# Late work of VectorE offered later, gate rows on GpSimd's queue, and p of group 3 scaled in the f stage

## The chip, the cores and the metric

The kernel runs on one core of a Trainium2 chip. The metric is the device time of one execution in microseconds (us). Three runs of the kernel before gave a median of 733.19 us (730.4 to 735.96).

## The reference

Two blocks read the same x (2048 tokens of 640 features) and are mixed by a gate of each token:

```python
g = sigmoid((x * gate_w).sum(-1))                      # one number per token
q, k, v = x @ wqkv                                     # 32 heads of 20
pq, pk = phi(q), phi(k)       # phi(t) = where(t > 0, t + 1, exp(t)) + 1e-6
kv = sum_s pk[s] v[s]^T ;  z = sum_s pk[s]             # per head
o = (pq @ kv) / (pq . z + 1e-6)
a = o @ wo
b = (sigmoid(x @ w_gate) * (x @ w_up)) @ w_down        # 1536 wide
out = g * a + (1 - g) * b
```

All of it is float32. The kernel gets that accuracy from split operands: each operand is a high part and a low part, and a product is three matmuls (lines 417 to 419), with a single one here and there (line 428).

## The kernel before

Tokens are handled in four groups of 512 (0 to 3), features in chunks of 128. "p" is phi(q) without its 1e-6, kept in DRAM as p_dram (128 features x 5 chunks x 4 groups x 512 tokens). kv and wo are multiplied together early into one 640 x 640 matrix M, so that the first block is a = M^T (p + 1e-6) scaled, per token and head, by the factor g / (pq . z + 1e-6).

Stages in the order of time: the k side (to about 145 us), the q side of groups 2 and 3, the gated unit of groups 2 and 3 (an "f stage"; twelve steps f, each 128 wide), the q side of groups 0 and 1, the f stage of groups 0 and 1 (some 450 to 645 us, `f_phase(0, ...)`), and the tail (from some 645 us), which forms M^T p for groups 2 and 3, then for 0 and 1, adds the gated unit's share and stores the result.

In the second f stage VectorE also does work that no matmul of that stage needs:

- `queue_dens` (lines 1575 to 1631) finds the factors, first for groups 2 and 3 (queued at step 2), then for 0 and 1 (at step 7). For each group it loads the five chunks of p (tile pden), sums p z into the tile fac (`one`), stores that in den_dram, loads it back turned so that heads lie along partitions (`turn_in`, four loads a group, which also loads the gate row gs), adds the parts, takes the reciprocal and multiplies by the gate (`factor`), stores the result in fac_dram, and loads it back spread over the 128 feature rows (`turn_out`, four loads a group). In the kernel before, the gate rows and the spreading loads are issued on SyncE's queue (SP), the rest on GpSimd's (POOL).
- `queue_m` forms the high and low parts of M (tiles mr, mt) and stores them through GpSimd's queue; its next loads of M (mr from m_dram) go on SyncE's queue.
- `queue_e` (lines 1435 to 1447) makes three small corrections of a step's weights (tile ws, 128 x 128 each).

In the tail `load_p` brings p of a group back from p_dram, `queue_scale` multiplies each chunk by the factor (`pq_scale`, one VectorE instruction of 128 x 512 a chunk), `queue_pq` splits it in a high part (ScalarE) and a low part (VectorE), and `queue_pt` forms sums of four chunks and splits those too. `queue_seed` puts the gated unit's share times 1 - g (tile omg) into a PSUM tile (dd or rot), on top of which the matmuls add. `load_m(1)` brings three of the ten pieces of M.

The order of the work is not written out by hand where it is queued: `Order` keeps an estimate of TensorE's, ScalarE's and VectorE's time while the program is written, and after each block of matmuls `fill` takes from its queues what is ready and fits (lists in the order urgent, streams, items, lazy, chain, spare; `chain` holds `queue_dens`, `spare` holds `queue_m`). Ready is what `ready()` says: for a transfer, the landing that `Rings` estimates for it. `DEN_LAG` (5.0) is added to that estimate in some places. `need` emits a queued piece at once. So a piece is emitted where the estimate says its data has landed; on the chip each engine runs its instructions strictly in that order, and an instruction whose data is late holds everything behind it on its engine. A tile name has a fixed number of buffers, so a load waits until the earlier user of its buffer is done. All vector, scalar and DMA instructions stand in helpers, so that their lines are those of the helpers: 433 ScalarE, 437, 441, 443 to 448 VectorE, 374 DMA.

Of the kernel before, what the change touches and what calls it, by code (L numbers as in the profile page):

```python
# [10 lines left out]
OP = mybir.AluOpType  # L11
# [3 lines left out]
P = 128  # L15
S, D, F = 2048, 640, 1536
H, DH = 32, 20
KC = D // P
FC = F // P
LAST = FC // 2 - 1  # L20
TG = 512
# [7 lines left out]
EPS = 1e-6  # L29
# [285 lines left out]
DEN_LAG = 5.0  # L315
# [65 lines left out]
def v_cost(w):  # L381
    return 0.07 + w / 960

@with_exitstack
def gated_mix_kernel(ctx: ExitStack, tc: tile.TileContext, x0, xt, xn, wk, wv, wo, wst_q, wst_f, out_t):
# [6 lines left out]
    order = Order()  # L392
# [46 lines left out]
    def vec3(out, a, scalar, b, op0, op1, after=""):  # L439
        order.on_vec(width(out), after, 1.0, out, a, b)  # L440
        nc.vector.scalar_tensor_tensor(out, a, scalar, b, op0=op0, op1=op1)
# [17 lines left out]
    def add(out, a, b, after=""):  # L459
        vec2(out, a, b, OP.add, after)  # L460
# [792 lines left out]
    def tt(name, dt=F32, shape=(P, TG)):  # L1253
        return pw.tile(list(shape), dt, name=name, tag="t", bufs=4)
# [180 lines left out]
    def queue_e(f):  # L1435

        n = ("f", 0, f)
        d, u = EW[f, "d"], EW[f, "u"]
        dh, dl = d[:, :P], d[:, P:]
        uh, ul = (W[n, 1][c][:, 2 * P:] for c in range(2))  # L1440

        def fn():
            vec3(u[:, :P], f32(dh), -1 / UP, f32(ul), OP.mult, OP.add)
            vec3(u[:, P:], f32(ul), UP, f32(uh), OP.mult, OP.add)
            vec3(dl, f32(dh), 1 / UP, f32(dl), OP.mult, OP.add)
        order.add(0, 3 * v_cost(P), fn, ("e", f), lambda: max(order.when(d), order.when(WT[n, 1])),
                  stream=("e", f), due=order.due((0, f, 3)))

    def queue_et(late):
# [112 lines left out]
    def gate_store():  # L1562
# [9 lines left out]
                              t[b * H:b * H + n, 1])  # L1572
        sp.dma_start(gate_rep, gate_dram[0].rearrange("(i o p) -> i o p", o=1, p=P).broadcast_to([n, H, P]))

    def queue_dens(*gs2):

        nonlocal fac
        if "f" in EF:
            EF.pop("f")
            fac = fac_tile()  # L1580
        st = {}

        def load(g, u):
            if u < KC:
                st[g, u] = tt("pden")
                gp.dma_start(st[g, u], p_dram[:, u, g])
                st["at", g, u] = lambda: order.when(st[g, u])

        def one(g, u):
            td = fac[:, g]  # L1590
            if u == 0:
                vec1(td, st[g, u], zcol[:, 0:1], zeps[:, 0:1], OP.mult, OP.add)
            else:
                vec3(td, st[g, u], zcol[:, u:u + 1], td, OP.mult, OP.add)
            load(g, u + 2)
            if u == KC - 1:
                gp.dma_start(den_dram[:, g], td)
                st["at", g, u + 1] = lambda: order.when(den_dram[:, g])

        def turn_in(g):  # L1600
            for j in range(4):
                js = slice(j * H, (j + 1) * H)
                gp.dma_start(fac[js, g].rearrange("h (d c) -> h d c", c=P),
                                  den_dram[:, g, j * P:(j + 1) * P].rearrange("(d h) c -> h d c", h=H))
            st[g, "gs"] = tt("gs")[:, :P]
            sp.dma_start(st[g, "gs"], gate_rep[4 * g:4 * g + 4].rearrange("i h c -> (i h) c"))
            st["at", g, KC + 1] = lambda: max(order.when(fac[:, g]), order.when(st[g, "gs"]))

        def factor(g):
            td = fac[:, g]  # L1610
            q = td[:, :P]
            add(td[:, :2 * P], td[:, :2 * P], td[:, 2 * P:])
            add(q, q, td[:, P:2 * P])
            order.on_vec(5 * P, "")
            nc.vector.reciprocal(q, q)
            vec2(q, q, st[g, "gs"], OP.mult)
            gp.dma_start(fac_dram[:, g], q)
            st["at", g, KC + 2] = lambda: order.when(fac_dram[:, g])

        def turn_out(g):  # L1620
            for d in range(4):
                sp.dma_start(fac[d * H:(d + 1) * H, g].rearrange("h (j c) -> h j c", c=P),
                                  fac_dram[:, g].rearrange("(j h) c -> h j c", h=H))
        order.add(0, 0, lambda: [load(g, u) for u in range(2) for g in gs2], chain=True)
        for u in range(KC):
            for g in gs2:
                order.add(0, v_cost(TG), lambda g=g, u=u: one(g, u), None, lambda g=g, u=u: st["at", g, u]() + DEN_LAG, chain=True)
        for n, (v, fn) in enumerate(((0, turn_in), (2.0, factor), (0, turn_out))):
            for g in gs2:
                order.add(0, v, lambda g=g, fn=fn: fn(g), ("fac", g) if n == 2 else None,  # L1630
                          lambda g=g, n=n: st["at", g, KC + n](), chain=True)

    sp.t = max(sp.t, gp.cell[0])
    load_w()
# [457 lines left out]
    OMG = {}  # L2092
# [527 lines left out]
    def load_m(i):  # L2620

        while any(it[3] == "m" for it in order.spare) or order.pend:
            order.need("m")
            order._flush()
        n = (0, 7, 10)
        t = (wf_tile, ws_tile)[i]().rearrange("p a b -> p (a b)")[:, :(n[i + 1] - n[i]) * D]
        for j0, j1 in ((0, 4), (4, 7), (7, 10))[2 * i:2 + i]:
            sp.dma_start(f32(t[:, (j0 - n[i]) * D:(j1 - n[i]) * D]),
                         mp_dram.rearrange("p a b c -> p (a b c)")[:, j0 * D:j1 * D])
        for j in range(n[i], n[i + 1]):  # L2630
            MHL[divmod(j, 2)] = t[:, (j - n[i]) * D:(j - n[i] + 1) * D]
# [23 lines left out]
    def load_p(g):  # L2655

        if g == groups[0]:
            PL[g] = [tt("pl") for _ in range(KC - 1)]
            PL[g].append(f32(wu_tile()).rearrange("p a b -> p (a b)")[:, :TG])
            for u in range(KC):  # L2660
                sp.dma_start(PL[g][u], p_dram[:, u, g])
        else:
            PL[g], PL[g, "t"] = [], []
            for u in range(0, KC, 2):
                t = (x2_tile if g == groups[1] else h_tile)(dt=F32)
                w = min(2, KC - u)
                sp.dma_start(t[:, :w], p_dram[:, u:u + w, g])
                PL[g] += [t[:, i] for i in range(w)]
                PL[g, "t"].append(t)
        PL[g, "at"] = lambda: max(order.when(t) for t in PL[g])  # L2670
# [26 lines left out]
            ST[-1] = n = n()  # L2697
        return n

    def pq_scale(g, u):  # L2700
        p = PL[g][u]
        vec3(p, p, EPS, fac[:, g], OP.add, OP.mult)

    def pq_tiles(g):

        t = [x2_tile("pq", F32R) for _ in range({2: 4, 3: 2}.get(g, KC))]
# [7 lines left out]
    def queue_scale(g, lazy=False):  # L2714
        order.need(("fac", g), False)
        for u in range(KC):
            order.add(0, v_cost(TG), lambda u=u: pq_scale(g, u), ("sc", g), lambda: PL[g, "at"](), lazy=lazy)

    def queue_pq(g):

# [48 lines left out]
        vec2(ps, BL[g][o], OMG[g], OP.mult)  # L2769

    def b_at(g, o):
        return max(order.when(BL[g][o]), order.when(OMG[g]) if g in OMG else 1e9)

    def queue_seed(g, o, tag):
        order.add(0, v_cost(TG), lambda: seed_b(g, o, tag), ("b", g, o), lambda: b_at(g, o), first=True)
# [153 lines left out]
    pq_tiles(2)  # L2929
    queue_pq(2)  # L2930
    load_p(3)
    load_m(1)
    pq_tiles(3)
    queue_scale(3)
    queue_pq(3)
    load_b(2)
    load_omg(3)
    load_b(3)
    load_b(0)
# [105 lines left out]
```

## Time and profile before

| | us |
|---|---|
| median of three runs | 733.19 |
| the profiled execution's own time | 734.18 |
| its span, first to last instruction | 732.5 |
| TensorE busy (98% of the span) | 721.5 |
| VectorE busy (80%) | 589.2 |
| ScalarE busy (50%) | 366.1 |
| GpSimd busy (16%) | 118.0 |

Some 1.7 us of the execution lie outside the span. The profile names TensorE's matmuls PE, its weight loads PEld, VectorE DVE, ScalarE ACT, GpSimd POOL and SyncE SP; SPq and POOLq are the DMA queues of the last two. A row of the timeline has start, duration, engine, line, operation, output and inputs with their shape, and in brackets the engine's idle time before it and what ended that. Matmuls of 512 columns start some 0.23 us apart, while a row shows each as 0.39 us long, because they are pipelined. The granted clock of TensorE (PEclk) is 1.00 at full speed.

### The profile page before, as it was taken

The numbers are of one execution on the slowest core, as the hardware profiler recorded it, in microseconds if no ns is written. First come the engines' busy times: TensorE is split into PE (matmuls) and PEld (weight loads), VectorE is DVE, ScalarE is ACT, GpSimd is POOL, SyncE is SP. The second block draws the span as 40 slices with busy tenths as digits, with TensorE's granted clock in tenths as the row PEclk, the third lists the DMA queues.
The fourth block names the chain that finished last, engine by engine and source line by source line (L and its number), as shares of the span: only waits on it lengthen the run. The fifth ranks groups of instructions, "written<-read, shape, count | busy, mean of one in ns | idle before, by whom it ended". The sixth has DMA issues, their size and how long they took to land.

```text
span 732.5 us, 9922 instructions
## 1 busy us (share of the span) xinstructions
PE 721.5 (98%) x3401; PEld 607.3 (83%) x3401; DVE 589.2 (80%) x1045; ACT 366.1 (50%) x682; POOL 118.0 (16%) x199
## 2 busy tenths in 40 slices
PE   9999999999999999999999999998999999999898
PEld 8999999888888888888888888886788888887676
DVE  4988878987777889888998886665776888689886
ACT  5764749267557644444456762363332333335351
POOL 0311111113212211211121122013001131000200
PEclk9999999999999999999999999999999999999999
DMA  8474658698787856657688787889588897779623
GB/s 269 116 205 112 177 137 259 158 326 297 278 323 258 308 205 230 244 221 263 246 330 277 218 287 271 325 283 316 190 250 296 284 323 247 256 287 330 124 42 130
DMA packets 75657, 177.60 MB, mean 242 GB/s; under 512 B 12266, under 2 KB 34170, under 8 KB 73430
## 3 DMA queue, kind: packets, MB, share of 16 engines
q1 hardware_dynamic: 55654, 104.03, 43.5%
q0 software_dynamic: 19664, 72.70, 29.0%
q8 instruction: 27, 0.44, 0.2%
q10 hardware_dynamic: 288, 0.23, 0.1%
q14 instruction: 24, 0.20, 0.1%
HBM read 104.62 MB, written 67.33 MB: 235 GB/s over the span
## 4 chain that ended last, share of the span: by engine, by line
PE 92%; DVE 3%; DMA 2%; ACT 1%; issue 1%; POOL 0%; SPq 0%; DVEq 0%; POOLq 0%; ACTq 0%
PE ch L418 10%; PE ch L419 10%; PE ch L417 10%; PE cc L418 7%; PE cc L419 7%; PE cc L417 7%; PE dd L417 7%; PE dd L418 7%; PE dd L419 7%; PE rot L419 5%; PE rot L418 5%; PE rot L417 5%; PE ch L428 1%; PE cc L428 1%; DMA fac<-den_dram 1%; DMA omg<-gate_dram 1%
## 5 line engine op out<-in xcount | busy, mean ns | idle before, releaser
L437 DVE TENSOR_TENSOR hf<-c,hf 128x512 fp32r<-128x512 f32 x77 | 52.6, 687 | 26.0 <-ACT hf L433 25.5
L433 ACT ACTIVATE hf<-c 128x512 fp32r<-128x512 f32 (+1 forms) x79 | 48.8, 625 | 39.6 <-DVE c L437 39.6
L433 ACT ACTIVATE c<-ch 128x512 f32<-128x512 f32 x43 | 25.7, 597 | 77.8 <-PE ch L428 56.9
L417 PE MATMUL ch<-xth,ws 128*128 128x512 f32 x108 | 42.2, 391 | 0.0
L419 PE MATMUL ch<-xth,ws 128*128 128x512 f32 x108 | 42.1, 390 | 0.0
L418 PE MATMUL ch<-xtl,ws 128*128 128x512 f32 x108 | 42.1, 389 | 0.0
L437 DVE TENSOR_TENSOR tb<-rot,tb 128x512 f32<-128x512 f32 x60 | 39.0, 684 | 1.9 <-PE rot L419 1.9
L437 DVE TENSOR_TENSOR c<-cc,c 128x512 f32<-128x512 f32 x38 | 26.2, 688 | 17.0 <-ACT c L433 10.1
L437 DVE TENSOR_TENSOR c<-c,c 128x512 f32<-128x512 f32 x48 | 33.0, 688 | 2.6 <-ACT c L433 2.0
L437 DVE TENSOR_TENSOR tb<-dd,tb 128x512 f32<-128x512 f32 x41 | 28.1, 686 | 8.3 <-PE dd L419 8.3
L433 ACT ACTIVATE dd<-ch 128x512 f32<-128x512 f32 x22 | 12.8, 583 | 36.2 <-PE ch L428 20.4
L433 ACT ACTIVATE c<-dd 128x512 f32<-128x512 f32 x21 | 12.5, 597 | 35.6 <-PE dd L428 17.0
L417 PE MATMUL dd<-xrh,wg 128*128 128x512 f32 x73 | 28.7, 394 | 1.5 <-ACT dd L433 1.5
L437 DVE TENSOR_TENSOR wst<-wst 128x256 f32<-128x256 f32 (+2 forms) x69 | 27.4, 412 | 1.4
L418 PE MATMUL dd<-xrl,wg 128*128 128x512 f32 x73 | 28.4, 390 | 0.0
L419 PE MATMUL dd<-xrh,wg 128*128 128x512 f32 x73 | 28.4, 389 | 0.0
L417 PE MATMUL cc<-xbh,ws 128*128 128x512 f32 x71 | 27.6, 389 | 0.0
L418 PE MATMUL cc<-xbl,ws 128*128 128x512 f32 x71 | 27.6, 389 | 0.0
L419 PE MATMUL cc<-xbh,ws 128*128 128x512 f32 x71 | 27.6, 389 | 0.0
L433 ACT ACTIVATE c<-c 128x512 f32<-128x512 f32 x31 | 19.5, 628 | 10.5 <-DVE c L437 10.2
L433 ACT ACTIVATE cx<-ch 128x512 f32<-128x512 f32 x16 | 9.6, 597 | 29.1 <-PE ch L419 28.9
L419 PEld LDWEIGHTS ch<-xth,ws 128*128 128x128 f32 x108 | 20.3, 188 | 4.5 <-DVE ws L437 0.3
(755 smaller groups left out, 2403.2 us busy)
## 6 DMA issues: line engine op xcount, KB each, us to landing
wf<-ws POOLq DMA_DIRECT2D x12, 1152.0 KB, 7.7
wst<-wst_f SPq DMA_DIRECT2D x12, 640.0 KB, 4.9
wf<-wg POOLq DMA_DIRECT2D x12, 640.0 KB, 6.8
wd<-wd POOLq DMA_DIRECT2D x12, 640.0 KB, 8.1
wg<-wf SPq DMA_DIRECT2D x12, 640.0 KB, 6.2
wf<-wd SPq DMA_DIRECT2D x10, 640.0 KB, 7.8
ws<-wf SPq DMA_DIRECT2D x23, 256.0 KB, 4.8
xnst<-xn SPq DMA_DIRECT2D x16, 320.0 KB, 4.1
```

What stands on the lines that cost most here:

```text
L417: nc.tensor.matmul(out, l_hi, r_hi, start=first, stop=False, skip_group_check=True)
L418: nc.tensor.matmul(out, l_hi, r_lo, start=False, stop=False, skip_group_check=True)
L419: nc.tensor.matmul(out, l_lo, r_hi, start=False, stop=last, skip_group_check=True)
L428: nc.tensor.matmul(out, w, x, start=False, stop=n == len(singles) - 1, skip_group_check=True)
L433: nc.scalar.activation(out, src, fn, **kw)
L437: nc.vector.tensor_tensor(out, a, b, op=op)
```

## The change

Four things are changed:

1. Three ready times are put later: `queue_e` by 5.0 us of the estimate, the first step of `factor` by 5.0, and the seeds (`b_at`) by 2.5 behind their omg. `factor` is cut in two: the additions (`factor`) and then reciprocal, product and store (`turn_over`), each queued for both groups in turn.
2. The gate rows gs and the spreading loads of `turn_out` are issued on GpSimd's queue, no longer on SyncE's.
3. For group 3 the five chunks of p are loaded again in the f stage once the factor is there (four into pden tiles, the fifth into the part of fac that later serves group 0), multiplied by the factor, and stored back to p_dram through GpSimd's queue (`scale`). `load_p(3)` then loads p already scaled, and the tail's `queue_scale(3)` is gone.
4. `load_m(1)` is issued behind `load_b(2)`, no longer ahead of it.

```diff
@@ queue_e
-        order.add(0, 3 * v_cost(P), fn, ("e", f), lambda: max(order.when(d), order.when(WT[n, 1])),
+        order.add(0, 3 * v_cost(P), fn, ("e", f), lambda: max(order.when(d), order.when(WT[n, 1])) + DEN_LAG,
                   stream=("e", f), due=order.due((0, f, 3)))
@@ ahead of queue_dens
+    scaled = (3,)
+
+    def pq_scale(p, g):
+        vec3(p, p, EPS, fac[:, g], OP.add, OP.mult)
@@ queue_dens
-        def load(g, u):
+        def load(g, u, t=None):
             if u < KC:
-                st[g, u] = tt("pden")
+                st[g, u] = tt("pden") if t is None else t
                 gp.dma_start(st[g, u], p_dram[:, u, g])
                 st["at", g, u] = lambda: order.when(st[g, u])
...
-            sp.dma_start(st[g, "gs"], gate_rep[4 * g:4 * g + 4].rearrange("i h c -> (i h) c"))
+            gp.dma_start(st[g, "gs"], gate_rep[4 * g:4 * g + 4].rearrange("i h c -> (i h) c"))
...
             add(td[:, :2 * P], td[:, :2 * P], td[:, 2 * P:])
             add(q, q, td[:, P:2 * P])
+
+        def turn_over(g):
+            q = fac[:, g, :P]
             order.on_vec(5 * P, "")
             nc.vector.reciprocal(q, q)
             vec2(q, q, st[g, "gs"], OP.mult)
             gp.dma_start(fac_dram[:, g], q)
-            st["at", g, KC + 2] = lambda: order.when(fac_dram[:, g])
+            st["at", g, KC + 3] = lambda: order.when(fac_dram[:, g])
 
         def turn_out(g):
             for d in range(4):
-                sp.dma_start(fac[d * H:(d + 1) * H, g].rearrange("h (j c) -> h j c", c=P),
+                gp.dma_start(fac[d * H:(d + 1) * H, g].rearrange("h (j c) -> h j c", c=P),
                                   fac_dram[:, g].rearrange("(j h) c -> h j c", h=H))
+        def scale(g, u):
+            t = st[g, u]
+            pq_scale(t, g)
+            gp.dma_start(p_dram[:, u, g], t)
+
+        def scale_at(g, u):
+            return max(order.when(st[g, u]), order.when(fac[:, g])) + DEN_LAG
+
...
-        for n, (v, fn) in enumerate(((0, turn_in), (2.0, factor), (0, turn_out))):
+        for g in gs2:
+            st["at", g, KC + 2] = lambda: 0.0
+        for n, (v, fn) in enumerate(((0, turn_in), (0.6, factor), (0.9, turn_over), (0, turn_out))):
             for g in gs2:
-                order.add(0, v, lambda g=g, fn=fn: fn(g), ("fac", g) if n == 2 else None,
-                          lambda g=g, n=n: st["at", g, KC + n](), chain=True)
+                order.add(0, v, lambda g=g, fn=fn: fn(g), ("fac", g) if n == 3 else None,
+                          lambda g=g, n=n: st["at", g, KC + n]() + (DEN_LAG if n == 1 else 0.0), chain=True)
+        for g in gs2:
+            if g in scaled:
+                order.add(0, 0, lambda g=g: [load(g, u, fac[:, 0] if u > 3 else None) for u in range(KC)], ("sc", g), chain=True)
+                for u in range(KC):
+                    order.add(0, v_cost(TG), lambda g=g, u=u: scale(g, u), ("sc", g), lambda g=g, u=u: scale_at(g, u), chain=True)
@@ load_p
+            if g in scaled:
+                order.need(("sc", g), False)
@@ b_at
-        return max(order.when(BL[g][o]), order.when(OMG[g]) if g in OMG else 1e9)
+        return max(order.when(BL[g][o]), order.when(OMG[g]) + DEN_LAG / 2 if g in OMG else 1e9)
@@ the tail
     load_p(3)
-    load_m(1)
     pq_tiles(3)
-    queue_scale(3)
     queue_pq(3)
     load_b(2)
+    load_m(1)
```

TensorE's order of instructions is unchanged. Three places show how the others move.

VectorE where it forms the factors of groups 2 and 3, before (c and hf are tiles of the gated unit, fac and gs belong to the factors, mt and mr to M):

```order
L437 TENSOR_TENSOR c_4618<-ch_4587,c_4618 128x512
L437 TENSOR_TENSOR hf<-c_4519,hf 128x512
L437 TENSOR_TENSOR fac<-fac 128x256
L437 TENSOR_TENSOR fac<-fac 128x128
L1615 RECIPROCAL fac<-fac 128x128
L437 TENSOR_TENSOR fac<-fac,gs 128x128
L437 TENSOR_TENSOR c_4658<-cc_4693,c_4658 128x512
L437 TENSOR_TENSOR mt<-mr,mt 128x640
L437 TENSOR_TENSOR mr<-mr 128x2x128 x2
```

and now:

```order
L437 TENSOR_TENSOR c_4841<-ch_4776,c_4841 128x512
L437 TENSOR_TENSOR fac<-fac 128x256
L437 TENSOR_TENSOR fac<-fac 128x128
L437 TENSOR_TENSOR fac<-fac 128x256
L437 TENSOR_TENSOR fac<-fac 128x128
L441 SCALAR_TENSOR_TENSOR ws<-ws,wu 128x128
L441 SCALAR_TENSOR_TENSOR ws<-wu 128x128
L441 SCALAR_TENSOR_TENSOR ws<-ws 128x128
L1623 RECIPROCAL fac<-fac 128x128
L437 TENSOR_TENSOR fac<-fac,gs 128x128
L437 TENSOR_TENSOR c_4857<-cc_4872,c_4857 128x512
L1623 RECIPROCAL fac<-fac 128x128
```

The factor of group 2 stood behind the c of step 4's ch product; now both groups' factors stand one step later, behind the c of step 5's ch product. In the kernel before, group 3's factor came by itself some 35 us later.

VectorE in the tail, where groups 0 and 1 begin, before (hf holds p of groups 0 and 1, pq its low parts, dd and rot are the seeded PSUM tiles):

```order
L441 SCALAR_TENSOR_TENSOR hf<-hf,fac 128x512 x8
L437 TENSOR_TENSOR mt<-ch_6204,mt 128x512
L437 TENSOR_TENSOR dd_6423<-tb,omg 128x512
L437 TENSOR_TENSOR dd_6425<-tb,omg 128x512
L437 TENSOR_TENSOR rot_6427<-tb,omg 128x512
L441 SCALAR_TENSOR_TENSOR hf<-hf,fac 128x512
L437 TENSOR_TENSOR st<-cc_6390,st 128x512
L441 SCALAR_TENSOR_TENSOR hf<-hf,fac 128x512
L437 TENSOR_TENSOR pq<-hf,pq 128x512 x10
```

and now:

```order
L441 SCALAR_TENSOR_TENSOR hf<-hf,fac 128x512 x7
L437 TENSOR_TENSOR pq<-hf,pq 128x512 x2
L437 TENSOR_TENSOR mt<-ch_6225,mt 128x512
L437 TENSOR_TENSOR pq<-hf,pq 128x512 x2
L437 TENSOR_TENSOR st<-cc_6409,st 128x512
L437 TENSOR_TENSOR pq<-hf,pq 128x512
L437 TENSOR_TENSOR dd_6465<-tb,omg 128x512
L437 TENSOR_TENSOR dd_6467<-tb,omg 128x512
L437 TENSOR_TENSOR rot_6478<-tb,omg 128x512
```

The three seeds now stand behind all ten scalings and five low parts, where they stood ahead of two scalings and every low part.

GpSimd's queue in the f stage, before:

```order
L374 DMA den_dram<-fac 128x512
L374 DMA mp_dram<-mt 128x1280
L374 DMA den_dram<-fac 128x512
L374 DMA fac<-den_dram 32x4x128 x8
L374 DMA fac_dram<-fac 128x128
L374 DMA mp_dram<-mt 128x1280
L374 DMA ms_dram<-mt 128x2x512 x2
L374 DMA fac_dram<-fac 128x128
```

and now:

```order
L374 DMA den_dram<-fac 128x512 x2
L374 DMA mp_dram<-mt 128x1280
L374 DMA fac<-den_dram 32x4x128 x4
L374 DMA gs<-gate_rep 128x128
L374 DMA fac<-den_dram 32x4x128 x4
L374 DMA gs<-gate_rep 128x128
L374 DMA fac_dram<-fac 128x128 x2
L374 DMA fac<-fac_dram 32x4x128 x8
L374 DMA pden<-p_dram 128x512 x4
L374 DMA fac<-p_dram 128x512
L374 DMA mp_dram<-mt 128x1280
L374 DMA p_dram<-pden 128x512 x4
```

The eight spreading loads, two gate rows, the five loads of p and their stores have come into this queue, between the stores of M.

More of the change, by code (lines that the diff above doesn't have):

```diff
@@ L2698, in st_tile @@
         return n
-    def pq_scale(g, u):
-        p = PL[g][u]
-        vec3(p, p, EPS, fac[:, g], OP.add, OP.mult)
     def pq_tiles(g):
@@ L2716, in queue_scale @@
         for u in range(KC):
-            order.add(0, v_cost(TG), lambda u=u: pq_scale(g, u), ("sc", g), lambda: PL[g, "at"](), lazy=lazy)
+            order.add(0, v_cost(TG), lambda u=u: pq_scale(PL[g][u], g), ("sc", g), lambda: PL[g, "at"](), lazy=lazy)
     def queue_pq(g):
```

## The prediction

> **What bounds the kernel now.** The page's first line and its busy times come first:
>
> ```profile
> span 732.5 us, 9922 instructions
> PE 721.5 (98%) x3401; PEld 607.3 (83%) x3401; DVE 589.2 (80%) x1045; ACT 366.1 (50%) x682; POOL 118.0 (16%) x199
> ```
>
> PE is the bound, and its instructions stay as they are, in kind and order. The change can save only what PE loses to stops and to a lower clock. The view of waits for PE alone, from 440 us on, where the change begins (waiter <- releaser: us in total, times, longest):
>
> ```profile
> PE ch L418 <- DVE pq L437: 2.9, 1, 2.9
> PE dd L417 <- ACT dd L433: 1.7, 2, 1.5
> PE ch L417 <- ACT c L433: 1.4, 1, 1.4
> PE cc L418 <- DVE pt L437: 0.2, 1, 0.2
> PE dd L417 <- DVE dd L437: 0.2, 1, 0.2
> ```
>
> That is 6.4 us in six stops. PE's timeline shows where, and what a stop costs beyond its bracket:
>
> ```profile
> 508.13 0.50 PE L417 MATMUL ch<-xth,wu 128*128 128x512 f32 x1 [1.45 <-ACT c L433]
> 509.86 0.39 PE L428 MATMUL ch<-ws,wu 128*128 128x512 f32 x1
> 511.71 0.50 PE L417 MATMUL dd<-xrh,wg 128*128 128x512 f32 x1 [1.47 <-ACT dd L433]
> ...
> 691.82 0.39 PE L417 MATMUL ch<-pq,wf 128*128 128x512 f32 x1
> 695.06 0.50 PE L418 MATMUL ch<-pq,wf 128*128 128x512 f32 x1 [2.86 <-DVE pq L437]
> 695.40 0.40 PE L419 MATMUL ch<-pq,wf 128*128 128x512 f32 x1
> ```
>
> From 691.82 to 695.06 are 3.24 us where 0.23 is the pitch: 3.01 lost; the next start comes 0.34 later, another 0.11. A stop so costs its idle time plus 0.26. Six cost 6.4 + 6 x 0.26 = 8.0. The clock follows (windows: us, busy and count of PE, PEld, DVE, ACT, POOL, then PEclk, DMA share, GB/s):
>
> ```profile
> 695.87:699.51 3.64, 3.64 (x10) 2.86 (x9) 2.84 (x5) 1.71 (x4) 0.00 (x0) 0.53 0.85 137
> 560.00:640.00 80.00, 80.00 (x354) 66.00 (x353) 64.66 (x116) 26.05 (x47) 13.03 (x23) 1.00 0.80 273
> ```
>
> The ten matmuls of the first row span nine pitches, 9 x 0.227 = 2.04 at full clock; 1.6 is lost. The second row shows a stretch with nothing to win. All that can go is 8.0 + 1.6 = 9.6 us.
>
> The Trainium skill ("TensorE: Matmul & The Clock Gate", What's actually happening) says that the gate halves the clock after an idle window of about 3.4 us. Here the granted clock fell after an idle time of 2.86; by that threshold the 1.6 would not be the stop's, and the sum below would end 1.6 higher.
>
> **Part one: the factors later.** What released PE at 508 and 511 was ScalarE, which VectorE had held up. The chain of waits, and VectorE's timeline:
>
> ```profile
> 496.71 7.53 DMA fac<-den_dram
> 504.26 0.44 DVE fac L437
> ```
>
> ```profile
> 493.28 0.74 DVE L441 SCALAR_TENSOR_TENSOR fac<-pden,zcol,fac 128x512 f32<-128x512 f32 x1
> 504.26 0.75 DVE L437 TENSOR_TENSOR fac<-fac 128x256 f32<-128x256 f32 x2 [6.45 <-DMA fac<-den_dram]
> ```
>
> VectorE stood 6.45 us at the factor's first addition, with the c and hf of two steps behind it. That cost PE three stops (the c row and the two dd): 1.4 + 1.7 + 3 x 0.26 = 3.9. So about 2.5 of the 6.45 were free; I use that below.
>
> In the new order both den_dram stores stand ahead of M's store on GpSimd's queue, and the loads behind it start at some 493. Tile fac's view prices them (duration min/median/max in ns, first and last start):
>
> ```profile
> L374 POOL DMA_DIRECT2D fac<-den_dram x16: 549/549/576, 495.1 to 601.0; - x16
> L374 SPq DMA_DIRECT2D fac<-fac_dram x16: 325/382/634, 536.3 to 620.3; - x16
> L441 DVE SCALAR_TENSOR_TENSOR pl<-pl,fac x9: 681/685/687, 641.3 to 665.6; 128x512 f32<-128x512 f32 x9
> ```
>
> Eight loads and two gate rows x 0.55 = 5.5, so the last is issued at 498.5 and lands, at the chain's 7.53, at 506. The addition now stands behind the c of the next step's ch. Its product is the matmul of 509.86, which without the first stop comes 1.45 + 0.11 earlier, at 508.3, and ends at 508.7; c takes 0.6: 509.3. That leaves 3 us, so I count 3.9 gained. Three corrections (`queue_e`) stand there too; nothing in these rows makes PE wait for them, so 0, and at most a stop of 0.3.
>
> **Part two: p of group 3 scaled in the f stage.** The queue's prices (KB each, median us from issue to landing):
>
> ```profile
> pden<-p_dram POOLq DMA_DIRECT2D x20, 256.0 KB, 5.5
> fac<-den_dram POOLq DMA_DIRECT2D x16, 64.0 KB, 5.6
> fac<-fac_dram SPq DMA_DIRECT2D x16, 64.0 KB, 5.1
> fac_dram<-fac POOLq DMA_DIRECT2D x4, 64.0 KB, 4.1
> bl<-b_dram SPq DMA_DIRECT2D x3, 256.0 KB, 12.2
> ```
>
> Both factors, each of two additions, a reciprocal and a product, are done at about 515. Store: +4.1 = 519. Eight spreading loads on GpSimd's queue: + 8 x 0.55 = 523.5 for the last issue, +5.6 = 529 (at 7.53: 531). The loads of p behind them, +5.5, land at 529 to 531. VectorE comes to the first scaling a little ahead of this tb, less the 3.9 gained:
>
> ```profile
> 532.98 0.69 DVE L437 TENSOR_TENSOR tb<-dd,tb 128x512 f32<-128x512 f32 x1 [0.84 <-PE dd L419]
> 536.83 0.69 DVE L437 TENSOR_TENSOR c<-ch,c 128x512 f32<-128x512 f32 x1 [0.52 <-PE ch L428]
> 540.46 0.69 DVE L437 TENSOR_TENSOR c<-cc,c 128x512 f32<-128x512 f32 x1 [0.36 <-PE cc L428]
> 543.25 0.69 DVE L437 TENSOR_TENSOR hf<-c,hf 128x512 fp32r<-128x512 f32 x1 [2.10 <-ACT hf L433]
> ```
>
> So it is wanted at about 529, there at 529 to 531: a wait of 0 to 2. The five scalings add 5 x 0.61 (the pitch inside a run of them; 0.685 is a row's length) = 3.0, against 0.84 + 0.52 + 0.36 + 2.10 = 3.8 of VectorE's idle time there. A wait of up to 2.5 was free by part one. Cost taken 0, with 0 to 1.5 as its bounds (2 of wait plus 3.0 of work, less 3.8, is 1.2, and a restart 0.26). The transfers fit, by the DMA share in the windows where they fall:
>
> ```profile
> 524.00:528.00 4.00, 4.00 (x19) 3.32 (x18) 3.08 (x8) 1.12 (x2) 0.00 (x0) 1.00 0.21 70
> 528.00:532.00 4.00, 4.00 (x19) 3.32 (x18) 4.00 (x7) 0.00 (x0) 0.00 (x0) 1.00 0.34 120
> ```
>
> **Part three: the tail.** Times here are on the clock of before; part one's 3.9 moves everything alike. The chain, VectorE's and ScalarE's timeline:
>
> ```profile
> 683.16 7.45 DMA omg<-gate_dram
> 690.71 1.30 DVE dd L437 x2
> ```
>
> ```profile
> 682.61 4.90 DVE L441 SCALAR_TENSOR_TENSOR hf<-hf,fac 128x512 f32<-128x512 f32 x8
> 690.71 1.30 DVE L437 TENSOR_TENSOR dd<-tb,omg 128x512 f32<-128x512 f32 x2 [2.01 <-DMA omg<-gate_dram]
> ```
>
> ```profile
> 687.07 1.14 ACT L433 ACTIVATE pq<-hf 128x512 fp32r<-128x512 f32 x2
> ```
>
> Before, VectorE waited 2.01 for omg, then seeded, scaled twice more, and only then formed the low part (pq) for which PE stopped 2.86 us. Now five scalings, 3.0 us, are gone from its queue, and the low parts stand ahead of the seeds. The scalings end about 685. ScalarE's high parts come from 687.07, the first ended at 687.6; VectorE's two low parts, 0.6 each, at 688.9. PE wants the second at 692.0, so 3 us are spare, even if PE comes 0.9 earlier. The seeds then end near 693 behind five more instructions; dd's first matmul comes some 3.5 us after 691.8 less that 0.9, at 694.4. omg, issued on SP behind a store that waits for VectorE, moves ahead with it and lands 3 earlier, near 687.6. So this stop goes, 2.9 + 0.26 = 3.1, and the clock's 1.6 with it. The two small ones, 2 x (0.2 + 0.26) = 0.9, hang on the same VectorE being 3 us ahead; I count half of them.
>
> `load_m(1)` behind the last bl: PE uses ws at
>
> ```profile
> 663.73 0.39 PE L419 MATMUL dd<-pq,ws 128*128 128x512 f32 x1
> 640.00:665.00 25.00, 24.82 (x110) 20.24 (x109) 21.76 (x36) 10.05 (x18) 0.00 (x0) 1.00 0.81 293
> ```
>
> The 960 KB and the bls are the same bytes in another order at a share of 0.81; the last of them landed about when the first small stop ended, 1 to 2 us ahead of 663.73. Cost 0, bounded by 0 and 2. SP loses 20 issues of some 0.38 (7.6 us), but PE waited for no load of its: gain 0.
>
> **The sum.** 734.18 - 3.9 - 3.1 - 1.6 - 0.5 = 725.1. The profiled execution lies 1.0 over the median of the runs, so on the median's ground 724.1; I take 724.5.
>
> **The rivals.**
> - *The last stop stays* (0.20). For it: omg, seeds and scalings are close together, and another late transfer can take omg's place. Against it: 3 us spare. 724.5 + 3.1 + 1.6 = 729.2.
> - *The f stage takes back what it gave* (0.13): VectorE waits at the first scaling as it did at 504, because the chain of store, spreading loads and p ends past 532. For it: 529 to 531 is not early. Against it: 2.5 of such a wait were free. 724.5 + 3.9 = 728.4.
> - *GpSimd's queue is late: slower* (0.06). If store, spreading loads and p each take what bl took on a loaded stretch, 12.2 for 4.1, 5.6 and 5.5, the first p is 21 late; with 2.5 free and VectorE standing, PE loses about 19: 724.5 + 19 = 743.5. It decides for "slower" only from a lateness of some 18.5 (16 us of loss bring 740.5). Against it: the share of 0.21 and 0.34 there. The Trainium skill ("SBUF — State Buffer", A bandwidth-pool intuition that's wrong) gives such a mechanism: GpSimd's descriptors wait for VectorE's shared port, 3100 ns for 620. By it the 15 added issues ahead of the scaling would be some 37 us late, an estimate, and the time some 35 longer. Tile fac's row of sixteen issues at 549 to 576 ns, beside a VectorE that is 80% busy, does not show it, so it gets no more than this rival's chance.
> - *Nothing is won* (0.05): the stops are this execution's own, or come back elsewhere: 733.
>
> **How the numbers follow.** My forecast has 0.56. About 1%, 7.3 us, is what a measurement of this kernel can tell from no change: below 725.9 or above 740.5. The forecast's own spread is 722 (all small stops gone, and a run somewhat under the median) to 727 (1.5 of the f stage's bound and a small stop); of its 0.56 some 0.45 lie below 725.9. The rest of it, the first two rivals and the fourth make 0.49 of no change, the third 0.06 of slower. The range reaches from 722 to the first rival with the f stage's bound, 729.2 + 1.5 = 730.7: 731.
>
> **What would show it.** Right: no bracket on PE near 504 to 520; no DVE wait over 2.5 at fac<-fac or at the first p scaling near 529; PEclk 1.00 in the tail; pq low parts ended before PE's ch. Wrong: a bracket on PE behind c or dd near 530 to 540 (second rival), one at the tail's ch or dd with omg or mt as the cause (first), POOL issues well over 0.55 us (third).

## The result and the profile after

The changed kernel takes 723.61 us (median of four runs, 723.36 to 723.78) against 733.88 for the kernel before in the same comparison; the ratio is 0.9867, with a 95% interval of 0.9839 to 0.9895. It is 1.3% faster. The forecast was 724.5, in a range of 722 to 731. The profiled execution took 723.69 against 734.18 before: 10.5 us less.

The first line and the busy times of the page after:

```profile
span 722.0 us, 9930 instructions
PE 717.6 (99%) x3401; PEld 606.1 (84%) x3401; DVE 587.9 (81%) x1045; ACT 365.4 (51%) x682; POOL 135.1 (19%) x229
```

The view of waits has no line for PE after 440 us any more, where before it had five. PE's timeline at the two places that had the large stops, and at a third:

```profile
506.08 0.39 PE L417 MATMUL ch<-xth,wu 128*128 128x512 f32 x1
...
507.89 0.39 PE L417 MATMUL dd<-xrh,wg 128*128 128x512 f32 x1
...
585.26 0.39 PE L419 MATMUL ch<-xth,ws 128*128 128x512 f32 x1
585.77 0.50 PE L428 MATMUL ch<-ws 128*128 128x512 f32 x1
586.11 0.39 PE L417 MATMUL dd<-hf,wf 128*128 128x512 f32 x1
...
686.64 0.39 PE L417 MATMUL ch<-pq,wf 128*128 128x512 f32 x1
686.87 0.39 PE L418 MATMUL ch<-pq,wf 128*128 128x512 f32 x1
687.10 0.39 PE L419 MATMUL ch<-pq,wf 128*128 128x512 f32 x1
```

A pitch is the usual distance of two starts, 0.23 us. From 506.08 to 507.89 are eight pitches without a bracket, where before there were 3.58 us between the same two matmuls (508.13 and 511.71). At 686.87, where PE had stood for 2.86 us, one start follows the other at 0.23. At 585.77 there is a stop that is new: 0.51 between starts, then 0.34.

PE's order is the same in both kernels, so the starts of the same matmul can be subtracted, and each step of that difference is a stop, or a stretch of lowered clock, that came or went:

| place (time before) | PE's gain, us |
|---|---|
| the three stops, 506 to 520 | 1.60 + 0.12 + 1.62 + 0.11 + 0.40 + 0.10 = 3.95 |
| the stop in the tail, 695 | 3.01 + 0.11 = 3.12 |
| the half clock behind it, 696 to 699.5 | 1.62 |
| small stops: 662, 674, 676, 708 | 0.47 + 0.21 + 0.42 + 0.64 = 1.74 |
| new: 590 (585.77 after), 712 | -0.39 - 0.22 = -0.61 |
| ahead of 440 us, where the programs do the same | 0.49 |

That is 10.3 of the 10.5. The last row lies ahead of the change and is taken as a difference between two executions; without it the change gave 9.8. The cause of the new 0.22 at 712 was not followed.

VectorE's timeline and GpSimd's, at the places that the prediction named:

```profile
509.42 1.40 DVE L437 TENSOR_TENSOR fac<-fac 128x256 f32<-128x256 f32 x4
...
528.65 0.68 DVE L441 SCALAR_TENSOR_TENSOR pden<-pden,fac 128x512 f32<-128x512 f32 x1
...
682.52 1.29 DVE L437 TENSOR_TENSOR pq<-hf,pq 128x512 fp32r<-128x512 f32 x2 [1.69 <-ACT pq L433]
...
686.73 1.30 DVE L437 TENSOR_TENSOR dd<-tb,omg 128x512 f32<-128x512 f32 x2
```

```profile
517.10 2.22 POOL L374 DMA_DIRECT2D fac<-fac_dram  x4 [1.86 <-DMA fac_dram<-fac]
521.81 2.18 POOL L374 DMA_DIRECT2D fac<-fac_dram  x4 [2.49 <-DMA fac_dram<-fac]
523.98 2.18 POOL L374 DMA_DIRECT2D pden<-p_dram  x4
```

The factor's additions, the first scaling and the seeds have no bracket: nothing late stands at VectorE's head any more. The two low parts of the tail end at 683.8, 3.1 us ahead of the matmul of 686.87 that wants the second. The windows:

```profile
524.00:528.00 4.00, 4.00 (x19) 3.33 (x18) 3.93 (x8) 0.17 (x1) 3.18 (x6) 1.00 0.99 340
690.00:710.00 20.00, 20.00 (x88) 16.26 (x88) 19.51 (x33) 8.67 (x17) 0.00 (x0) 1.00 0.28 90
```

The DMA share where p of group 3 is fetched is 0.99, where the same 4 us had 0.21 before (and the next 4, which PE now reaches some 4 us earlier, 0.34), and PE stayed busy for all of those 4 us. PEclk in the tail is 1.00.

### The profile page after: what moved, and what is told of

Same layout as the page of the kernel before. It is cut to its first block, busy times and chain, and to the rows that moved or that the text cites. A ratio compares the mean times of both kernels' runs of the same rounds, so it can differ in the third digit from the quotient of the medians.

```text
span 722.0 us, 9930 instructions
## 1 busy us (share of the span) xinstructions
PE 717.6 (99%) x3401; PEld 606.1 (84%) x3401; DVE 587.9 (81%) x1045; ACT 365.4 (51%) x682; POOL 135.1 (19%) x229
## 4 chain that ended last, share of the span: by engine, by line
PE 99%; DVE 0%; ACT 0%; issue 0%; ACTq 0%
PE ch L417 11%; PE ch L418 11%; PE ch L419 11%; PE cc L417 8%; PE cc L418 8%; PE cc L419 8%; PE dd L417 7%; PE dd L418 7%; PE dd L419 7%; PE rot L419 6%; PE rot L418 6%; PE rot L417 6%; PE ch L428 2%; PE cc L428 1%; PE rot L1726 1%; PE dd L428 1%
## 5 line engine op out<-in xcount | busy, mean ns | idle before, releaser
L437 DVE TENSOR_TENSOR wst<-wst 128x256 f32<-128x256 f32 (+2 forms) x69 | 27.4, 412 | 1.4
L374 POOL DMA_DIRECT2D wf<-ws x12 | 6.5, 544 | 95.9 <-DVE ws L437 84.9
```

Of the source, the lines that this page charges most:

```text
L374: return self.engine.dma_start(out, src, **kw)
L437: nc.vector.tensor_tensor(out, a, b, op=op)
```

## Experiments

Each kernel is the one before or the changed one with a part undone or done alone. PE's order is the same in all of them, so a step in the difference of starts is a stop or a lowered clock. The times:

| kernel | median, us | ratio to before, 95% interval |
|---|---|---|
| changed kernel | 723.61 | 0.9867 [0.9839, 0.9895] |
| before + later factor | 729.4 | 0.9957 [0.9938, 0.9977] |
| before + later seeds | 728.47 | 0.9944 [0.9925, 0.9963] |
| before + both of these | 724.66 | 0.9903 [0.9883, 0.9923] |
| changed, scaling in the tail, seeds not later | 731.1 | 0.9978 [0.9963, 0.9993] |
| changed, seeds not later | 724.47 | 0.9892 [0.9877, 0.9907] |
| changed, factor not later | 723.78 | 0.9880 [0.9862, 0.9897] |
| changed, corrections not later | 722.69 | 0.9873 [0.9858, 0.9888] |
| changed, neither of these later | 723.21 | 0.9877 [0.9862, 0.9892] |
| changed, load_m(1) first | 724.99 | 0.9901 [0.9883, 0.9919] |
| changed, scaling offered 5.0 earlier | 735.12 | 1.0046 [1.0032, 1.0061] |
| changed, rows on SyncE's queue | 733.6 | 1.0023 [1.0013, 1.0033] |
| changed, spreading loads four times | 775.98 | 1.0600 [1.0575, 1.0625] |

The kernel before had medians of 732.1 to 733.9 in these comparisons, so the ratios compare better than the medians do.

### One stop each: the factor alone, the seeds alone

The first kernel is the one before with `factor` cut in two and its first step 5.0 later; the second is the one before with the seeds later:

```diff
+                          lambda g=g, n=n: st["at", g, KC + n]() + (DEN_LAG if n == 1 else 0.0), chain=True)
```

```diff
+        return max(order.when(BL[g][o]), order.when(OMG[g]) + DEN_LAG / 2 if g in OMG else 1e9)
```

> The kernel before with one part of the change alone: the factor's first step put 5.0 later and cut in two (both groups' additions, then reciprocal and product). Seeds, corrections, scaling of group 3, gate rows, spreading loads and load_m(1) stand as before. Theory (VectorE stands behind the late turned-in sums): the three stops of PE at 506 to 519 us go, 3.9 us; the tail keeps its stop of some 2.9 us and the lowered clock; time 734.2 - 3.9 = 730.3. Rival (the stops at 506 to 519 come and go by execution and have no such cause): they are there in some form, 733 to 734. A second rival: the wait only moves to the later place and PE stops there, 733 to 734 with a bracket behind fac<-fac near 510 to 513.

> The kernel before with one part alone: the seeds' ready time 2.5 behind their omg. All ten scalings of group 3 and 0, 1 stay in the tail, the stops at 506 to 519 stay. Its order of VectorE puts the scalings and two low parts of p ahead of the first seed that waits for omg. Theory: order alone takes the tail's stop away, because ten scalings from 682.6 at 0.61 end at 688.7 and the low part at 689.9, ahead of the 692.0 at which PE wants it; 734.2 - 3.1 - 1.6 = 729.5, the stops at 506 to 519 unchanged. Rival (the five scalings of group 3 in the tail are what makes VectorE late): the stop stays in the tail at 1 us or more, 732 to 734.

The waits of PE in the kernel with the later factor, and the window behind its first line:

```profile
PE ch L418 <- DVE pq L437: 2.4, 1, 2.4
```

```profile
690.08:693.90 3.82, 3.82 (x11) 2.99 (x10) 2.98 (x6) 1.63 (x3) 0.41 (x1) 0.55 0.95 137
```

The waits of PE in the kernel with the later seeds, and VectorE's timeline in its tail:

```profile
PE dd L417 <- ACT dd L433: 1.7, 2, 1.5
PE ch L417 <- ACT c L433: 1.7, 1, 1.7
```

```profile
681.95 5.50 DVE L441 SCALAR_TENSOR_TENSOR hf<-hf,fac 128x512 f32<-128x512 f32 x9
687.36 0.69 DVE L437 TENSOR_TENSOR pq<-hf,pq 128x512 fp32r<-128x512 f32 x1
...
689.16 0.70 DVE L437 TENSOR_TENSOR dd<-tb,omg 128x512 f32<-128x512 f32 x1
```

Each took away its own stop and left the other: 729.4 for 730.3 expected, 728.5 for 729.5. The stops at 506 and the one in the tail have separate causes, and in both VectorE stands at a late transfer with work behind it that PE wants. They are not accidents of one execution either: each kernel that keeps such a place shows the same stop. In the second kernel the scalings of group 3 are all still in the tail, and the low parts end in time, because no seed stands ahead of them.

### Both together, and which part of the change keeps the tail free

```diff
-    scaled = (3,)
+    scaled = ()
```

with `queue_scale(3)` back in the tail gives the second kernel below (the seeds' delay is taken out as well); the first is the one before with the two edits above; the third is the changed kernel without the seeds' delay.

> The kernel before with two parts of the change and nothing else: the factor later and cut in two, and the seeds 2.5 behind their omg. Group 3 is scaled in the tail as before, gate rows and spreading loads on SyncE's queue, corrections and load_m(1) as before. The factor alone gave 729.4 with the three stops at 506 to 519 gone, the seeds alone 728.5 with the tail's stop gone. Theory (VectorE's order is all, and the two are independent): both gone, 732.4 - 3.0 - 3.9 = 725.5 by the two measured differences, up to 1.5 over the changed kernel for the small stops that only the scaling, the queues or load_m(1) take away. Rival (the scaling of group 3 in the f stage is needed once the factor is late): the tail's stop is back at 1 us or more, 727 to 729.

> The changed kernel with the five scalings of group 3 back in the tail and the seeds' ready time as before; factor, corrections, gate rows, spreading loads and load_m(1) as changed. Theory: both things that kept the tail's stop away are gone, so it is back at 2 to 3 us behind omg or pq, with the lowered clock behind it: 723.6 + 3.1 + 1.6 = 728.3. Rival (the tail's stop went because all of the tail's transfers come earlier, by the queue and by load_m): no bracket of over 0.5 us in the tail, 723.6 to 724.5.

> The changed kernel with the seeds' ready time as before, all else as changed: the scaling of group 3 stays in the f stage. On VectorE two low parts of p then stand ahead of the first seed, and the other eight behind the third. Theory: without the five scalings VectorE is 3 us earlier, omg lands before it is wanted, and the tail's stop stays away by the scaling alone: 723.6 to 724.2, no bracket of over 0.5 us on PE. Rival (only the seeds' order took the stop away): it is back with the lowered clock, 727 to 728.3.

The one wait of PE that the view shows after 440 us, first in the kernel before with both edits, then in the changed kernel without the seeds' delay:

```profile
PE dd L417 <- DVE dd L437: 0.2, 1, 0.2
```

```profile
PE ch L417 <- DVE mt L437: 0.3, 1, 0.3
```

With neither scaling in the f stage nor later seeds, the waits of PE and VectorE's timeline:

```profile
PE ch L418 <- DVE pq L437: 4.1, 1, 4.1
PE ch L417 <- DMA ws<-wf: 0.9, 1, 0.9
```

```profile
687.70 1.30 DVE L437 TENSOR_TENSOR dd<-tb,omg 128x512 f32<-128x512 f32 x2 [3.23 <-DMA omg<-gate_dram]
```

So the stop in the tail is kept away twice over: by the seeds' place or by the five scalings that left. Either alone does it; without both it is back, and longer than before (4.1 for 2.86), because the seeds now stand 3.23 us at omg. The 0.9 at a weight load (near 549) was expected by neither theory. Two edits to the kernel before, without moving the scaling, give 724.66, most of what the whole change gives.

### What freed the factor

Three kernels take delays out of the changed kernel: the factor's, the corrections' (`queue_e`), and both.

```diff
-    ... + (DEN_LAG if n == 1 else 0.0), chain=True)
+    ... , chain=True)
```

```diff
-    lambda: max(order.when(d), order.when(WT[n, 1])) + DEN_LAG,
+    lambda: max(order.when(d), order.when(WT[n, 1])),
```

> The changed kernel with the factor's first step as early as before (no 5.0), all else as changed. Its first factor addition stands eight instructions earlier on VectorE, behind the c of step 4's cc product, at some 500 us; the loads it needs were issued from 493.0 on and, at 7.5, land at 500.5 to 502.7. Theory: VectorE waits 1 to 3 us there, of which about 2.5 are free for PE: 723.6 to 724.5, with a DVE bracket at fac<-fac and no or one small bracket on PE. Rival (the lag alone took the stops away): the stops at 506 to 519 are back, 3.9 us: 727.5.

> The changed kernel without the 5.0 on the corrections; the factor's 5.0 stays. GpSimd's queue has one den_dram store behind M's store again, as in the kernel before. Theory: the factor's additions, at 509, are behind the landing of the last load anyway (some 506), so no stop there; the one stop that is left in the changed kernel, 0.3 + 0.1 us at 585.8 behind a correction, goes: 723.2. Rival (the order of the den_dram stores is what freed the factor): a DVE wait of over 2 us at fac<-fac near 509 and 0.6 to 4 us of stops, 724 to 727.

> The changed kernel without the 5.0 on the factor and without the 5.0 on the corrections; the factor stays cut in two, all of the tail as changed. GpSimd's queue has again one den_dram store behind M's store, and VectorE's first factor addition stands one instruction later than in the kernel before, behind the c of step 4's cc product. Theory (either of the two delays keeps the factor's wait harmless, since taking the factor's alone cost nothing): with both gone VectorE waits from about 500.5 to 504, some 3.5 us, and PE loses 3.5 - 2.5 = 1 to 2: 724.6 to 725.6. Rival 1 (the cut into two steps or the queue for the gate rows did it): 723.6. Rival 2 (all of the stops are back): 727.5.

VectorE's timeline at the factor: without the factor's delay,

```profile
500.18 0.74 DVE L437 TENSOR_TENSOR fac<-fac 128x256 f32<-128x256 f32 x2
```

without the corrections' delay (the last sum, whose store follows M's again, and the additions),

```profile
492.50 0.74 DVE L441 SCALAR_TENSOR_TENSOR fac<-pden,zcol,fac 128x512 f32<-128x512 f32 x1
...
509.64 1.41 DVE L437 TENSOR_TENSOR fac<-fac 128x256 f32<-128x256 f32 x4
```

and without both, with PE's wait that follows:

```profile
503.12 0.75 DVE L437 TENSOR_TENSOR fac<-fac 128x256 f32<-128x256 f32 x2 [2.40 <-DMA fac<-den_dram]
```

```profile
PE dd L417 <- ACT dd L433: 0.4, 1, 0.4
```

Either delay alone leaves no bracket on VectorE. I had expected 1 to 3 us without the factor's; there are none, since the loads, issued from 493 on, were there at 500. With both gone the wait is 2.40, not 6.45, and costs PE 0.51 + 0.11 between starts. VectorE comes to the additions at 500.7 instead of 497.8, behind one more c, and the turned-in sums are there at 503.1 instead of 504.3: these two are the other 4 us. Which part of the change moved them, the cut of `factor` in two or the gate rows on GpSimd's queue, no run separates. The medians of 723.78 and 723.21 are not to be told from the changed kernel's.

Without the corrections' delay the new stop is gone as expected; PE's timeline there:

```profile
584.91 0.39 PE L419 MATMUL ch<-xth,ws 128*128 128x512 f32 x1
585.14 0.39 PE L428 MATMUL ch<-ws 128*128 128x512 f32 x1
```

0.23 between starts for 0.51 in the changed kernel, and the next start another 0.11 earlier: 0.4 us. Its 722.69 is the lowest median of all kernels, but its ratio, 0.9873, is not under the 0.9867 of the changed one: by time they can't be told apart, only by that place in the trace.

### The order of two loads

```diff
     load_p(3)
+    load_m(1)
     pq_tiles(3)
     queue_pq(3)
     load_b(2)
-    load_m(1)
```

> The changed kernel with load_m(1) ahead of load_b(2) again. Theory: the same bytes in another order; only the seeds of group 2 wait for bl, so the small stop at the first dd of the tail (0.34 + 0.11 in the kernel before, 0.5 with two parts alone) may be back: 723.6 to 724.1. Rival (the place of load_m is what freed the tail): brackets of 1 us or more between 655 and 690, 725 to 728.

PE's timeline at the first dd of the tail:

```profile
659.87 0.50 PE L417 MATMUL dd<-pq,wf 128*128 128x512 f32 x1 [1.09 <-DVE dd L437]
```

1.25 + 0.12 between starts, the only stop over 0.2: 1.4 us, more than the stop of the kernel before there (0.35 + 0.12), and above my 723.6 to 724.1 at 724.99. The rival's 1 us was right on the size, and its 725 nearly; but only this one bracket came back, so the place of load_m decides about the first seeds, not the tail. How it does so is not what my theory said. VectorE's seeds dd, in this kernel and then in the changed one:

```profile
659.12 1.30 DVE L437 TENSOR_TENSOR dd<-bl,omg 128x512 f32<-128x512 f32 x2
```

```profile
656.43 1.29 DVE L437 TENSOR_TENSOR dd<-bl,omg 128x512 f32<-128x512 f32 x2
```

They have no bracket, so VectorE does not wait for bl there: they stand behind two low parts and the seed of rot, which stand behind them in the changed kernel. It is again the order of VectorE that costs.

### The scaling offered earlier, and the rows on SyncE's queue

```diff
         def scale_at(g, u):
-            return max(order.when(st[g, u]), order.when(fac[:, g])) + DEN_LAG
+            return max(order.when(st[g, u]), order.when(fac[:, g]))
```

```diff
-            gp.dma_start(st[g, "gs"], ...
+            sp.dma_start(st[g, "gs"], ...
-                gp.dma_start(fac[d * H:(d + 1) * H, g] ...
+                sp.dma_start(fac[d * H:(d + 1) * H, g] ...
```

> The changed kernel with the scalings of group 3 offered 5.0 earlier. The first then stands four instructions further ahead on VectorE, at some 525 us, three others at 527, while its p lands at about 528. Theory (of a wait of VectorE in the f stage some 2.5 us are free): a wait of about 3 there costs PE 0.5 to 1: 724.0 to 724.6. Rival (nothing is free, or M's parts mt and mr that it pushes back are wanted): 726 to 727 with brackets on PE near 530.

> The changed kernel with gate rows and spreading loads back on SyncE's queue. The eight spreading loads of a pair then wait there for fac_dram ahead of weights. Theory (no weight was ever late for PE in the kernel before, which had them there): no change, 723.4 to 724.0, no bracket on PE behind a DMA; the first scaling of group 3 is released by p, not later than now. Rival (SyncE's queue held up weights): one or two brackets of 0.5 to 1 us behind ws or wu, 724.5 to 726.

Both kernels came out slower than the kernel before, and no theory had that; the rival of the first names M's parts, but with stops near 530 and at 726 to 727. The earlier scaling: VectorE's timeline, then PE's, then the chain of waits.

```profile
527.94 0.69 DVE L441 SCALAR_TENSOR_TENSOR pden<-pden,fac 128x512 f32<-128x512 f32 x1 [2.49 <-DMA fac<-fac_dram]
...
652.75 0.42 DVE L437 TENSOR_TENSOR mt<-mr,mt 128x256 fp32r<-128x256 f32 x1 [9.08 <-ACT mt L433]
```

```profile
529.89 0.50 PE L417 MATMUL rot<-hf,wf 128*128 128x512 f32 x1 [1.24 <-DVE tb L437]
...
653.30 0.79 PE L417 MATMUL dd<-hf,wg 128*128 128x512 f32 x1 [7.41 <-ACT hf L433]
```

```profile
643.51 8.69 DMA mp_dram<-mt
```

The wait that I had meant to buy is there, 2.49 us, and costs PE 1.41 + 0.11 between starts. The other 10 us are lost more than 100 us later: the last, narrow piece of M wants the tile mt, whose store was issued at 643.51 and took 8.69 us to land. ScalarE waits for the tile, VectorE for ScalarE's high part, the c and hf of the last step stand behind VectorE's instruction, and PE stands 7.41 us; a lowered clock follows, with starts 0.43 apart for 0.23 (10.1 lost in all between starts). The same with the rows on SyncE's queue: PE, VectorE and the chain.

```profile
652.40 0.79 PE L417 MATMUL dd<-hf,wg 128*128 128x512 f32 x1 [7.43 <-ACT hf L433]
```

```profile
651.86 0.42 DVE L437 TENSOR_TENSOR mt<-mr,mt 128x256 fp32r<-128x256 f32 x1 [9.11 <-ACT mt L433]
```

```profile
642.59 8.72 DMA mp_dram<-mt
```

In the changed kernel these two pieces of M lie far apart on VectorE:

```profile
622.27 0.82 DVE L437 TENSOR_TENSOR mt<-mr,mt 128x640 fp32r<-128x640 f32 x1
...
639.33 0.41 DVE L437 TENSOR_TENSOR mt<-mr,mt 128x256 fp32r<-128x256 f32 x1
```

The 640-wide piece is done at 623, its store was issued at 623.4, and ScalarE writes the tile for the last piece at 632.5 without a wait. In both slower kernels the planner (`Order` with its `fill`) put that piece some 20 us later (642.4 and 641.5), directly ahead of the last one. M stands in its last list, so I take it that what else is offered pushes it back. What PE lost is the store that the last piece then met. No matmul waited for a weight with the rows on SyncE's queue: in this the theory held, and that queue is not the cause. The edit moves M on VectorE all the same, and it can do that only by the planner's estimates, since they set the order. That the wait at the store is the loss is in the trace; why the planner shifts M by just that much was not followed through its estimates.

### A late queue

Every spreading load is issued four times (the same bytes again), and the first scaling is offered at once:

```diff
-            for d in range(4):
+            for d in list(range(4)) * 4:
...
         def scale_at(g, u):
-            return max(order.when(st[g, u]), order.when(fac[:, g])) + DEN_LAG
+            return 0.0
```

> The changed kernel with every spreading load issued four times (24 more issues for groups 2 and 3, the same bytes again, same result) and the first scaling of group 3 offered as early as its queue allows, so that VectorE stands at it, near 518, until the queue is through: 32 issues at 0.55 and two landings from 517, then p: about 541. It prices the rival of a late queue. Theory (a wait costs PE its length less 1 to 2 us): a wait of some 22 us on VectorE, 20 us lost on PE in that place, with the lowered clock after it: 745, and more if M's parts are pushed back so far that their stores meet the tail. Rival (most of it hides, as nothing of the scaling is wanted in that stage): under 735.

VectorE's timeline and PE's waits:

```profile
545.60 0.69 DVE L441 SCALAR_TENSOR_TENSOR pden<-pden,fac 128x512 f32<-128x512 f32 x1 [27.43 <-DMA pden<-p_dram]
```

```profile
PE dd L417 <- ACT hf L433: 23.6, 1, 23.6
PE dd L417 <- DVE tb L437: 23.2, 1, 23.2
```

The wait was 27.4 (22 expected) and cost PE 23.2 there and some 2 us of lowered clock. A second loss of that size, 23.6, came at M: its last three pieces stand close together there, and VectorE waits 16.64, 4.20 and 3.60 us (at 684.5, 689.4 and 694.3) for ScalarE, which waits for the stores of the pieces before them. The theory's 745 was short by that second stop, which its last clause had left open.

## Why the prediction was right, and where its steps were not

**What can be won.** The sum of all that could go was 9.6; 10.5 went, 0.5 of it ahead of the change. The large terms hold nearly to the digit: 3.9 and 3.95 at the factor, 3.1 and 3.12 in the tail, 1.6 and 1.62 for the clock. The term that was too small is that of the small stops: counted at 0.5 of 0.9, they gave 1.74. Two of them (674 and 676, 0.6 together) had no line in PE's waits and are seen only between the starts. The new stop at a correction, bounded at 0.3 in part one, cost 0.39, and another 0.22 came at 712. These misses partly cancel (1.2 more won, 0.6 newly lost), so that the total came nearer than its small terms is luck; that the large stops go, and why, is not.

**Part one** held: additions wanted at 509.3, at 509.42 with no wait. But the reason was one of several. With `factor` cut in two, its delay alone takes the three stops away, in the kernel before as in the changed one; in the changed kernel the earlier den_dram store does so without the delay; and with neither, 0.62 of the 3.95 is left.

**Part two** held in its own place: last spreading load issued at 523.5, measured 524.0; scaling wanted at 529, at 528.65 with no wait. In the kernel that asked some 3 us earlier the release came at 527.9, so some 0.7 us were spare; of the wait of 0 to 2 that I gave, none came. The step "a wait of up to 2.5 was free by part one" was wrong in size: 2.49 us at the scaling cost PE 1.5 (1.0 free), 2.40 at the factor cost 0.6 (1.8 free). How much is free belongs to the place, not to the stage. It did not matter, as there was no wait.

**Part three** held: low parts ended 3.1 us ahead of PE, forecast 3; the seeds 1.3 ahead, forecast 1.4. That the scalings were needed for it did not: with the low parts ahead of the seeds the five scalings could have stayed.

**load_m(1)**, taken at 0 with a cost of up to 2, is a gain: 1.4 us are lost without it. The bound of 2 had the size and the wrong sign. The gain holds beside the other parts of the change: in the kernel with the two edits alone, which has load_m(1) first, PE loses only 0.44 there.

**The step that failed** is "SP loses 20 issues ... PE waited for no load of its: gain 0". Moving those issues back costs 10 us, all of the gain. I had costed a queue move by the queue alone, and the second rival by the wait at the scaling alone (3.9); what decided was where the planner then puts M's last pieces, which stood nowhere in my sum. The changed kernel is on the good side of that, and as far as the prediction goes this is luck: M's last two pieces are 17 us apart, where these two neighbours have them one right behind the other, with a store of 8.7 us to wait for between them. My chance of 0.06 for slower rested on the lateness of GpSimd's queue; its price came out near (23.2 of a wait of 27.4, so 4 rather than 2.5 not felt), but a slower kernel was closer by another way.

## What to carry to other kernels

Where one engine is 98% busy and its order fixed, subtract the start times of the same instruction in two traces: the steps give every stop, those without a bracket too. A late transfer costs by what stands behind its instruction, so moving the instruction behind a few that are wanted sooner is worth as much as making the transfer early, and here two such moves (factor and seeds) gave 724.66 by themselves, most of the gain. When a planner sets the order, an edit is priced only when the places of the work in its lowest list are looked up too: the loss can lie 100 us from the edit.

## What the runs showed of the hardware

The granted clock fell to 0.55 behind a stop of 2.4 us, and it stayed at 1.00 behind stops of 1.7 and 1.5 that lay 3.6 us apart (the waits stand above, the last two in the kernel with the later seeds). Its clock in the window around them:

```profile
508.00:513.00 5.00, 3.46 (x14) 2.55 (x15) 4.80 (x10) 1.69 (x4) 0.46 (x1) 1.00 0.99 359
```

The Trainium skill ("TensorE: Matmul & The Clock Gate", What's actually happening) has an idle window of about 3.4 us; in these traces less was enough: each stop of 2.4 us or more in the stretch from 440 us on was followed by a lowered clock, none of 1.7 or less was by itself, and none lay between.

GpSimd issued its loads at the same pace beside a VectorE that was busy for 3.93 of 4 us (the window of 524 to 528 above, and four loads in 2.18 us from 523.98 on); tile fac's view of the changed kernel:

```profile
L374 POOL DMA_DIRECT2D fac<-fac_dram x16: 552/552/578, 517.1 to 619.4; - x16
```

The Trainium skill ("SBUF — State Buffer", A bandwidth-pool intuition that's wrong) measured its 3100 ns for 620 beside a tensor_copy of VectorE. VectorE's rows in that window are all TENSOR_TENSOR, so these kernels show no blocking beside that instruction and do not test the skill's case; the prediction's estimate of 37 us carried the figure over to instructions for which it is not given. And p, fetched at a DMA share of 0.99, was there in time for a scaling some 5 us behind its issue.
